# First stage of a split Fourier transform: one product over two batches, or four products in the quarters of PE

## The chip, the cores and the metric

The kernel runs on one core of a Trainium2 chip. The metric is the device time of one execution in microseconds. A core has TensorE (PE, matrix products into PSUM), VectorE (DVE), ScalarE (ACT), GpSimd (POOL) and SyncE (SP), each with an instruction queue of its own, and 16 DMA engines that the queues of SP, POOL and ACT feed. SBUF and PSUM have 128 partitions; PSUM has 8 banks of 512 f32 numbers per partition.

## The reference

```python
X = np.fft.fft(x, axis=1)            # x: (8, 3008, 256) f32
X = np.fft.fft(X, axis=2)
x = X.real.reshape(24064, 256)
h = x @ w_in                         # (256, 2048)
g = h * np.clip(h + 3.0, 0.0, 6.0) / 6.0
out = g @ w_out                      # (2048, 256)
```

## The kernel before

**The transform.** The sequence of 3008 = 47 x 64 is transformed in two stages: 47-point transforms down the columns n1 (first stage, `stage1`), then 64-point ones with the twiddle factors in the table (`stage2`). The transform over the 256 columns is folded into `w_in`. The 8 batches go in 4 pairs. Before the first stage the input is folded by symmetry (`fold`: rows with their partners, columns with theirs), so that 32 of the 64 values of n2 are left. They come in 8 chunks of 4 (`XC`); the last chunk (index 7, the first in the order of pair 0) also holds n2 = 0 and 32 and is computed from two half products.

**First stage.** A chunk's rows lie on 94 partitions (`PR`), the 47 values of n1 of the one batch under those of the other. The table `F` is block-diagonal, 94 x 96: its two 47 x 48 blocks give 24 frequencies with real and imaginary part for each batch (`PZ` = 96). `stage1(pr, c, i)` (lines 199 to 214) is one product of 94 x 96 with 512 columns, two values of n2; it is called for i = 0 and 1. `evict_z` has ScalarE copy each 96 x 512 result from PSUM to `z`, and behind the second one SP stores `z` to DRAM (`zd`, line 243). `turn_column` makes a copy with signs of one column of `z` and stores it to `zq` (257 to 261). For pair 0, `turned_column` computes this column by small products instead. `load_g` reads `zd` and `zq` back, batches on 64 partitions each, for `stage2`.

**Input.** POOL's queue loads a chunk: `load_forward` (line 150) 96 rows in one DMA, and `load_partners` (159) 96 rows of the reversed partners by an indirect DMA. For pair 0 VectorE folds, for the others POOL (lines 170 to 178).

**The start.** Pair 0's 8 chunks are loaded, folded, transformed and stored one after another (lines 685 to 703), each followed by a product with nothing to compute (`keep_awake`, 622). Of `zd` only the first sixth is stored at once (248); the rest waits in `later` and is stored by SP in the first eight steps (853). Then the weights are rebuilt from their stored form by all engines, and folded (593 to 610).

**The steady loop.** 384 steps (4 pairs x 12 chunks of output x 8). Step s issues, in this order on each queue: what `beside` has put at this step; `mlp1` of step s + 2 (line 337: 4 products into the PSUM tiles u and v; VectorE adds and gates at 342 to 358 and 382, ScalarE applies relu at 379); `combine` of step s + 1 (POOL, 396); and `mlp2` of step s (line 422: 7 products by a Strassen-like scheme). `beside(p)` puts the next pair's loads, folds and first-stage products at fixed steps: load at t, the folds at t + 3 and t + 5, the two products at t + 8 and t + 11, with t = 9c for chunk c (t = 8 + 8c beside pair 0). It also puts the second-stage products and `load_g` of this pair.

**Banks.** PSUM is divided by hand: four banks for the accumulators (`ps_a`), three in a ring for u, v and other short tiles (`ps_h`, tag `uv`), and one (`ps_d`, tag `d`) shared by first and second stage. In the start (`starting`) `bank` gives accumulator banks instead. The order of instructions is the program's own (`manual_schedule`); each engine works its queue off in order.

Of the kernel before, what the change touches and what calls it, by code (L numbers as in the profile page):

```python
# [58 lines left out]
def kernel(  # L59
# [17 lines left out]
    PR, PZ = 2 * N1, 4 * NK1  # L77
    XC = 4
# [32 lines left out]
    F = consts.tile([PR + 2, 6 * PZ], F32, name="F")  # L111
    FI = consts.tile([PR + 2, NP * NXC + 1], F32, name="FI")
    IX = consts.tile([PR + 2, NP * NXC], I32, name="IX")
# [19 lines left out]
    def x_tile(pr, c):  # L133
        pool, tag = (spool, "t") if pr.p == 0 and ORDER.index(c) % 3 == 2 else (xpool, "x")
        return pool.tile([PR + 2, XC, D], F32, tag=tag, name="xt")
# [8 lines left out]
    def load_forward(pr, c):  # L144
        xt = x_tile(pr, c)

        nr = PR + 2 if pr.p < NP - 1 else PR
        rows = x_pn[pr.p * PR:pr.p * PR + nr]
        n = XC if c < NXC - 1 else XC - 1
        nc.gpsimd.dma_start(out=xt[0:nr, 0:n, :], in_=rows[:, c * XC + 1:c * XC + 1 + n, :])  # L150
        if n < XC:
            nc.gpsimd.dma_start(out=xt[0:nr, n:XC, :], in_=rows[:, 0:1, :])
        pr.x[c] = xt

    def load_partners(pr, c):
        xr = x_tile(pr, c)
        pr.xr[c] = xr
        i = pr.p * NXC + c
        nc.gpsimd.indirect_dma_start(
            out=xr[:].rearrange("p n d -> p (n d)"), out_offset=None, in_=x_r,  # L160
            in_offset=bass.IndirectOffsetOnAxis(ap=IX[:, i:i + 1], axis=0),
        )

    def fold(pr, c, part, eng):
        xt, xr = pr.x[c][0:PR], pr.xr[c][0:PR]
        n = XC if c < NXC - 1 else XC - 1
        a, r = xt[:, 0:n, :], xr[:, XC - 1:(XC - 1 - n) if n < XC else None:-1, :]
        tt = eng.tensor_tensor
        if part == 0:
            tt(a[:, :, 1:P], a[:, :, 1:P], r[:, :, D - 1:P:-1], op=AL.add)  # L170
            tt(a[:, :, D - 1:P:-1], a[:, :, D - 1:P:-1], r[:, :, 1:P], op=AL.add)
            return
        y = ypool.tile([PR, XC + 1, D], F32, tag="y", name="y")
        pr.y[c] = y
        lo, hi = xt[:, :, 1:P], xt[:, :, D - 1:P:-1]
        tt(y[:, 0:XC, 1:P], lo, hi, op=AL.add)
        tt(y[:, 0:XC, P + 1:D], lo, hi, op=AL.subtract)
        tt(y[:, 0:n, 0:P + 1:P], a[:, :, 0:P + 1:P], r[:, :, 0:P + 1:P], op=AL.add)
        if n < XC:
            h = xr[:, 0, :]  # L180
            tt(y[:, XC, 1:P], h[:, 1:P], h[:, D - 1:P:-1], op=AL.add)
            tt(y[:, XC, P + 1:D], h[:, 1:P], h[:, D - 1:P:-1], op=AL.subtract)
            eng.tensor_copy(y[:, XC, 0:P + 1:P], h[:, 0:P + 1:P])
            eng.tensor_copy(y[:, n, 0:P + 1:P], xt[:, n, 0:P + 1:P])
        del pr.x[c], pr.xr[c]
# [13 lines left out]
    def stage1(pr, c, i):  # L199

        y = pr.y[c]
        pt = turned_column(pr, c, y) if pr.p == 0 and i == 0 else None
        ps = bank([P, 2, D], "ps1")
        if (c, i) == (NXC - 1, XC // 2 - 1):


            nc.tensor.matmul(ps[0:PZ, 0], F[0:PR, 0:PZ], y[:, 2 * i], start=True, stop=False, skip_group_check=True)
            for k, (j, cs) in enumerate([(XC - 1, slice(0, P + 1)), (XC, slice(0, P + 1)),
                                         (XC - 1, slice(P + 1, D)), (XC, slice(P + 1, D))]):
                nc.tensor.matmul(ps[0:PZ, 1, cs], F[0:PR, (k + 1) * PZ:(k + 2) * PZ], y[:, j, cs],  # L210
                                 start=False, stop=(k % 2 == 1), skip_group_check=True)
        else:
            nc.tensor.matmul(ps[0:PZ], F[0:PR, 0:PZ], y[:, 2 * i:2 * i + 2, :], start=True, stop=True)  # L213
        evict_z(pr, c, i, ps, pt)


    def turned_column(pr, c, y):
        n = XC if c < NXC - 1 else XC - 1
        pt = ps_h.tile([P, 2 * TB], F32, tag="uv", name="pt")
        nc.tensor.matmul(pt[0:PZ, 0:n], F[0:PR, 5 * PZ:6 * PZ], y[:, 0:n, P], start=True, stop=True)  # L220
        for k in range(2 if n < XC else 0):
            nc.tensor.matmul(pt[0:PZ, n:XC], F[0:PR, (k + 1) * PZ:(k + 2) * PZ], y[:, n + k, P:P + 1],
                             start=(k == 0), stop=(k == 1))
        return pt

    def evict_z(pr, c, i, ps, pt):
        if i == 0:
            k = ORDER.index(c) if pr.p == 0 else 0

            pool, tag = (zpool, "z") if k < 2 else (cpool, "c") if k < 5 else (qpool, "q") if k < 7 else (apool, "a")  # L230
            pr.z[c] = pool.tile([PZ, XC, DZ[pr.p > 0]], F32, tag=tag, name="z")
            if pr.zd is None:
                pr.zd = dpool.tile([NG, 2, 2 * KK, 2, NS, DZ[pr.p > 0]], F32, tag=f"zd{pr.p > 0}", name="zd")
                pr.zq = dpool.tile([NG, 2, 2 * KK, 2, NS], F32, tag="zq", name="zq") if pr.p > 0 else None
        z = pr.z[c]
        if pt is not None:
            nc.scalar.copy(z[:, :, D], pt[0:PZ, 0:XC])
        nc.scalar.copy(z[:, 2 * i:2 * i + 2, 0:D], ps[0:PZ])
        if i == XC // 2 - 1:
            zd = pr.zd[:].rearrange("g b k c n d -> (g b k c) n d")[:, c * XC:(c + 1) * XC, :]  # L240
            del pr.y[c], pr.z[c]
            if pr.p > 0:
                nc.sync.dma_start(out=zd, in_=z[:])
                turn_column(pr, c, z)
            else:

                n0 = PZ // NG
                nc.sync.dma_start(out=zd[0:n0], in_=z[0:n0])
                later.append((zd[n0:], z[n0:]))
# [4 lines left out]
    def turn_column(pr, c, z):  # L254
        n = XC if c < NXC - 1 else XC - 1
        zc = zpool.tile([PZ, XC], F32, tag="zc", bufs=4, name="zc")
        nc.scalar.activation(zc[:, 0:n], z[:, 0:n, P], AF.Identity, scale=FI[0:PZ, NP * NXC:])
        cs = slice(c * XC, c * XC + n)
        nc.sync.dma_start(out=pr.zq[:, :, :, ::-1, cs].rearrange("g b k c n -> (g b k) c n"), in_=zc[:, 0:n])
        if n < XC:  # L260
            nc.sync.dma_start(out=pr.zq[:, :, :, :, c * XC + n].rearrange("g b k c -> (g b k c)"), in_=z[:, n, P])


    def load_g(pr, gr):
        g = gpool.tile([P, 2 * KK, D + 1], F32, tag="g", name="g")
        gb = [g[b * N2:(b + 1) * N2] for b in range(2)]
        for b in range(2):
            nc.sync.dma_start(out=gb[b][:, :, 0:DZ[pr.p > 0]], in_=pr.zd[gr, b].rearrange("k c n d -> (c n) k d"))
        for b in range(2) if pr.p > 0 else ():
            nc.sync.dma_start(out=gb[b][:, :, D], in_=pr.zq[gr, b].rearrange("k c n -> (c n) k"))  # L270
        pr.g[gr] = g
# [356 lines left out]
    nc.sync.dma_start(out=FI[:], in_=c_stage1[:, 6 * PZ:])  # L628
    nc.sync.dma_start(out=F[:], in_=c_stage1[:, 0:6 * PZ])
# [57 lines left out]
    for k, c in enumerate(ORDER):  # L687
        for part in range(2):
            fold(first, c, part, nc.vector)
        for i in range(XC // 2):  # L690
            stage1(first, c, i)
# [47 lines left out]
    def beside(p):  # L739
        at = {}  # L740

        def put(t, f, *a):
            at.setdefault(t, []).append((f, a))
# [19 lines left out]
        if p + 1 < NP:  # L763
            nx = pairs[p + 1]
            for c in range(NXC):
# [4 lines left out]
                for i in range(XC // 2):  # L770
                    put(t + 8 + 3 * i, stage1, nx, c, i)
# [3 lines left out]
        return at  # L775
# [62 lines left out]
    for s, (p, ck, fc) in enumerate(steps):  # L838
        if ck == 0 and fc == 0:
            at = beside(p)  # L840
        for f, a in at.get(ck * NF + fc, ()):
            f(*a)
        if s < NF:
# [8 lines left out]
            for dst, src in later[2 * s:2 * s + 2]:  # L852
# [10 lines left out]
        else:  # L863
            if s + AHEAD < len(steps):
                mlp1(*chunk(s + AHEAD))
            if s + 1 < len(steps):
# [14 lines left out]
def _tables(B, S, D):  # L881
# [14 lines left out]
    f = np.zeros((2, N1, 6, 2, NK1, 2))  # L896
    for b in range(2):
        for i, (re, im) in enumerate([(co, si), (co, o), (o, co2), (si, o), (o, si2), (-si, co)]):
            f[b, :, i, b, :, 0], f[b, :, i, b, :, 1] = re, im
    f[:, :, 2:5:2] = f[:, ::-1, 2:5:2]  # L900
    f = f.reshape(2, N1, 6, 2, NK1 // 4, 4, 2).swapaxes(3, 4)
# [3 lines left out]
    rows = np.arange(2)[:, None] * N1 + np.arange(N1)[::-1]  # L905
    rows = (rows.reshape(-1, 1) + 2 * N1 * np.arange(B // 2)) * 2 * npc
    rows = rows[:, :, None] + 2 * npc - 1 - np.arange(npc)
    f = np.concatenate([f.reshape(2 * N1, -1), rows.reshape(2 * N1, -1)], axis=1)

    f = np.pad(f, ((0, 2), (0, 0)))  # L910
    f = np.concatenate([f, 1.0 - 2.0 * (np.arange(4 * NK1)[:, None] % 2)], axis=1)
# [47 lines left out]
```

## Time and profile before

| what | value |
|---|---|
| median of 3 runs | 1968.65 us (1968.22 to 1968.8) |
| profiled execution, its time | 1967.16 us |
| its span, first to last instruction | 1965.4 us |
| PE clock granted, mean | 0.999 |
| one step of the loop on PE (599.36 to 604.11) | 4.75 us |
| POOL: one load of x, one indirect load (median) | 0.548, 0.956 us |
| ScalarE: one copy of z | 0.582 us |
| data moved | 93.34 MB, mean 47 GB/s |

The busy time of an engine counts the time in which at least one of its instructions runs. PE's records overlap, since its ends are modelled with the way through the array, so the distance between starts tells what a product costs, and the mean length does not. `x120` for line 213 counts two records for each of 60 products. A group's last part is the idle time of its engine just before it, and what ended most of it. In an order of time, the first number is the start in the span, the second the length, with neighbours of one kind merged.

### The profile page before, as it was taken

The page shows a single profiled execution, that of the slowest core. Times are in us where ns is not written, and L with a number is a line of the kernel's source. Part 1 is how long each engine was busy: PE and PEld are TensorE (multiplying, and loading weights), DVE is VectorE, ACT ScalarE, POOL GpSimd, SP SyncE. Part 2 cuts the span into 40 slices and gives each one's busy share as a digit, 9 for nine tenths or more (in the row PEclk, how much of TensorE's full clock was granted, in tenths as well). Part 3 has the DMA queues.
Part 4 walks back from the last instruction along what each step waited for, and adds up shares of the span by engine and source line. Part 5 has one row for each costly group of instructions (what it writes and reads, how often), then busy time and mean ns, then how long its engine had stood idle before and what let it go on. Part 6 is the DMA issues. An engine that isn't in the chain of part 4 may idle for free.

```text
span 1965.4 us, 27617 instructions
## 1 busy us (share of the span) xinstructions
PE 1942.5 (99%) x9134; PEld 1671.3 (85%) x9134; DVE 1437.9 (73%) x2777; ACT 687.9 (35%) x1167; POOL 1399.7 (71%) x1593
## 2 busy tenths in 40 slices
PE   9999999999999999999999999999999999999997
PEld 4678888888998888888898888888889888888887
DVE  6876776767777777777787776777678777777776
ACT  5633333333333333333333333333333333333322
POOL 4077877876677877787668777778667667666764
PEclk9999999999999999999999999999999999999999
DMA  7521212211112122121211221112110101101000
GB/s 232 172 70 37 66 44 62 52 36 35 35 28 51 43 69 54 36 51 27 49 27 37 55 61 35 52 44 54 35 27 20 28 17 23 29 19 28 19 20 20
DMA packets 144701, 93.34 MB, mean 47 GB/s; under 512 B 116743, under 2 KB 130059, under 8 KB 144558
## 3 DMA queue, kind: packets, MB, share of 16 engines
q1 hardware_dynamic: 134294, 57.89, 12.2%
q0 software_dynamic: 9472, 33.49, 5.9%
q8 instruction: 72, 1.18, 0.3%
q14 instruction: 71, 0.58, 0.1%
q10 hardware_dynamic: 792, 0.20, 0.0%
HBM read 54.22 MB, written 37.32 MB: 47 GB/s over the span
## 4 chain that ended last, share of the span: by engine, by line
PE 93%; DVE 3%; DMA 1%; ACT 1%; issue 1%; SPq 0%; DVEq 0%; POOL 0%; ACTq 0%; POOLq 0%
PE acc L422 55%; PE v L337 16%; PE u L337 16%; PE ps L213 2%; PE ps L286 2%; DMA xt<-in_x_dram,IX 1%; DVE a L382 1%; PE acc L406 1%; DVE s L342 1%; ACT t L379 1%; PE spare L593 0%; DVE o L480 0%; DVE u L363 0%; ACT PM L532 0%; DMA T<-in_c_stage_dram 0%
## 5 line engine op out<-in xcount | busy, mean ns | idle before, releaser
L396 POOL TENSOR_TENSOR c<-a 128x512 f32<-128x512 f32 (+1 forms) x375 | 468.4, 1249 | 399.9 <-PE acc L422 335.4
L422 PE MATMUL acc<-c,G 128*128 128x256 f32 (+1 forms) x3008 | 696.9, 374 | 0.0
L379 ACT ACTIVATE t<-u,half 128x512 f32<-128x512 f32 (+1 forms) x384 | 261.3, 681 | 1099.3 <-DVE u L352 1019.6
L422 PEld LDWEIGHTS acc<-c,G 128*128 128x128 f32 x3008 | 565.4, 190 | 71.1
L342 DVE SCALAR_TENSOR_TENSOR s<-qn,WN,u 128x256 f32<-128x256 f32 (+1 forms) x768 | 330.3, 471 | 353.1 <-PE u L337 352.6
L422 PE MATMUL acc<-a,G 128*128 128x256 f32 (+1 forms) x2256 | 538.8, 374 | 0.0
L422 PEld LDWEIGHTS acc<-a,G 128*128 128x128 f32 x2256 | 423.3, 190 | 55.0
L337 PE MATMUL v<-q,W 127*128 127x256 f32 (+1 forms) x1536 | 389.0, 375 | 2.6 <-DVE a L382 2.6
L337 PE MATMUL u<-q,W 128*128 128x256 f32 (+1 forms) x1536 | 387.9, 375 | 0.0
L382 DVE SCALAR_TENSOR_TENSOR a<-t,u 128x512 f32<-128x512 f32 (+2 forms) x448 | 263.8, 601 | 103.0 <-ACT t L379 98.7
L337 PEld LDWEIGHTS u<-q,W 128*128 128x128 f32 x1536 | 285.8, 190 | 56.1 <-issue 15.8
L337 PEld LDWEIGHTS v<-q,W 127*128 127x128 f32 x1536 | 288.1, 190 | 42.8 <-ACT t L379 2.7
L396 POOL TENSOR_TENSOR c<-a,c 128x256 f32<-128x256 f32 (+1 forms) x375 | 268.8, 717 | 29.4
L396 POOL TENSOR_TENSOR c<-c,a 128x256 f32<-128x256 f32 (+1 forms) x375 | 268.3, 715 | 29.4
L352 DVE TENSOR_TENSOR u<-s,v 128x512 f32<-128x512 f32 x352 | 245.0, 696 | 37.0 <-DVE s L342 0.5
L382 DVE SCALAR_TENSOR_TENSOR a<-t,v 128x512 f32<-128x512 f32 (+1 forms) x480 | 263.7, 566 | 0.5 <-ACT t L379 0.4
L379 ACT ACTIVATE t<-v,half 128x512 f32<-128x512 f32 (+1 forms) x384 | 261.3, 681 | 0.6 <-PE acc L422 0.4
L354 DVE TENSOR_TENSOR v<-v,s 128x512 f32<-128x512 f32 x352 | 244.0, 693 | 0.0
L396 POOL TENSOR_TENSOR r<-w,e 128x256 f32<-128x256 f32 (+1 forms) x92 | 88.8, 986 | 3.6
L430 ACT ACTIVATE e<-acc 128x512 f32<-128x512 f32 (+2 forms) x186 | 84.6, 546 | 3.4 <-PE acc L422 3.3
L480 DVE STREAM_TRANSPOSE o<-r 128x256 f32<-128x256 f32 (+1 forms) x192 | 72.5, 415 | 0.2
L213 PE MATMUL ps<-y,F 94*96 94x512 f32 x120 | 61.3, 601 | 5.2 <-ACT q L289 5.2
(97 smaller groups left out, 794.8 us busy)
## 6 DMA issues: line engine op xcount, KB each, us to landing
out_dram<-o SPq DMA_DIRECT2D x746, 32.0 KB
zd<-z SPq DMA_DIRECT2D x24, 384.0 KB
g<-zd SPq DMA_DIRECT2D x36, 256.0 KB
xt<-in_x_dram POOLq DMA_DIRECT2D x21, 384.0 KB, 4.2
qn<-qd SPq DMA_DIRECT2D x19, 256.0 KB
st<-in_moe_w_in_dram POOLq DMA_DIRECT2D x8, 512.0 KB, 8.0
st<-in_moe_w_out_dram POOLq DMA_DIRECT2D x8, 512.0 KB, 5.6
g<-zd SPq DMA_DIRECT2D x12, 257.0 KB
```

The source lines that it names most:

```text
L213: nc.tensor.matmul(ps[0:PZ], F[0:PR, 0:PZ], y[:, 2 * i:2 * i + 2, :], start=True, stop=True)
L286: nc.tensor.matmul(ps[:, blk, u * P:n].rearrange("p (b k) -> p b k", b=2), g[:, kk, blk * (P + 1):blk * (P + 1) + P], T[:, :, gr, blk, kk, ...
L337: nc.tensor.matmul(ps[:, i, 0:nq], W1[r, blk, f * P:(f + 1) * P], q[r, blk, of:of + nq], start=True, stop=True)
L342: nc.vector.scalar_tensor_tensor(s[:, i, 0:nq], qn[:, of:of + nq], WN[:, f:f + 1], u[:, i, 0:nq], op0=AL.mult, op1=AL.add)
L352: nc.vector.tensor_tensor(u[:], s[:], v[:], op=AL.add)
L354: nc.vector.tensor_tensor(v[:], v[:], s[:], op=AL.subtract)
L379: nc.scalar.activation(t, h, AF.Relu, bias=half[:], scale=scale)
L382: nc.vector.scalar_tensor_tensor(dst, t, 1.0, h, op0=AL.min, op1=AL.mult)
L396: (eng or nc.gpsimd).tensor_tensor(out, in0, in1, op=AL.add)
L422: nc.tensor.matmul(ch.acc[i // 2][:, i % 2, 0:ch.n], G[:, i, fc, :], mv, start=(fc == 0 and i % 2 == 0), stop=(fc == NF - 1), skip_group_c ...
L430: nc.scalar.mul(ch.e[:, k:i + 1, 0:ch.n], ch.acc[i // 2][:, 0:i + 1 - k, 0:ch.n], 1.0 / WS)
L480: nc.vector.transpose(o[:, 0:n // DH, h], ch.r[:, m, h, 0:n].rearrange("p (j i) -> p j i", i=DH))
```

## The change

Each batch of a pair now lies on 64 partitions of its own (rows 0 to 46, and 64 to 110), and the table is the 47 x 48 block alone, once for each batch, padded to 64 columns. The first stage of a chunk is four products, two batches (b, by rows) times two halves of the chunk (h, by columns of the array): each takes 47 partitions and 64 columns, a quarter of PE, with 512 moving columns. Batch b has a PSUM bank of its own, in which half h fills 64 partitions. ScalarE still copies two results for each chunk, now 112 x 512 each, one for each batch. The second bank is a slot of the `uv` ring.

- `stage1` is called once for a chunk, at t + 8, and behind `mlp1` of the step where it was in front (`behind`).
- The forward load is two DMAs, 64 and 48 rows; the indirect load takes 112 rows (96 before). The 17 rows between the batches are loaded and folded but in no product.
- The stores of `z` are two for each chunk, one for each half, with pieces of two n2 (2 KB) in place of four; so are those of `zq` and the deferred ones in `later` (16 of 40 rows for 8 of 80; the same steps).
- `turned_column` is four small products for one. `zd` and `zq` have the batch in another place of their layout.

```diff
-    PR, PZ = 2 * N1, 4 * NK1
+    PB, PZ = P // 2, 2 * NK1
+    PX = PB + N1 + 1
...
+        for b in range(2):
+            i = 2 * pr.p + b
+            nr = N1 + 1 if i < B - 1 else N1
+            if b == 0:
+                nr = PB
+            rows, o = x_pn[i * N1:i * N1 + nr], xt[b * PB:b * PB + nr]
+            nc.gpsimd.dma_start(out=o[:, 0:n, :], in_=rows[:, c * XC + 1:c * XC + 1 + n, :])
...
-    def stage1(pr, c, i):
-        ps = bank([P, 2, D], "ps1")
...
-            nc.tensor.matmul(ps[0:PZ], F[0:PR, 0:PZ], y[:, 2 * i:2 * i + 2, :], start=True, stop=True)
-        evict_z(pr, c, i, ps, pt)
+    def stage1(pr, c):
+        y = pr.y[c]
+        pt = turned_column(pr, c, y) if pr.p == 0 else None
+        ps = [bank([P, 2, D], "ps1"),
+              bank([P, 2, D], "ps1") if starting[0] else ps_h.tile([P, 2, D], F32, tag="uv", name="ps1")]
+        for h in range(2):
+            last = (c, h) == (NXC - 1, 1)
+            for b in range(2):
+                n = 1 if last else 2
+                nc.tensor.matmul(ps[b][h * PB:(h + 1) * PB, 0:n], F[rows(b), 0:PB], y[rows(b), 2 * h:2 * h + n],
+                                 start=True, stop=not last, skip_group_check=last)
+            cosine, sine = slice(0, P + 1), slice(P + 1, D)
+            for k, (j, cs) in enumerate([(XC - 1, cosine), (XC, cosine), (XC - 1, sine), (XC, sine)] if last else ()):
+                for b in range(2):
+                    nc.tensor.matmul(ps[b][h * PB:(h + 1) * PB, 1, cs], table(k + 1, b), y[rows(b), j, cs],
+                                     start=False, stop=(k % 2 == 1), skip_group_check=True)
+        evict_z(pr, c, ps, pt)
+
+    def rows(b):
+        return slice(b * PB, b * PB + N1)
...
+        for b in range(2):
+            if pt is not None:
+                nc.scalar.copy(z[:, b, :, D], pt[b][0:PB + PZ, 0:2])
+            nc.scalar.copy(z[:, b, :, 0:D], ps[b][0:PB + PZ])
+        n0 = PZ // NG if pr.p == 0 else PZ
+        for h in range(2):
+            cs = slice(c * XC + 2 * h, c * XC + 2 * h + 2)
+            zd = pr.zd[:].rearrange("b g k c n d -> (g k c) b n d")[:, :, cs, :]
+            nc.sync.dma_start(out=zd[0:n0], in_=z[h * PB:h * PB + n0])
+            if n0 < PZ:
+                later.append((zd[n0:], z[h * PB + n0:h * PB + PZ]))
...
-                for i in range(XC // 2):
-                    put(t + 8 + 3 * i, stage1, nx, c, i)
+                put(t + 8, stage1, nx, c, at=behind)
...
-            for dst, src in later[2 * s:2 * s + 2]:
+            for dst, src in later[4 * s:4 * s + 4]:
...
             if s + AHEAD < len(steps):
                 mlp1(*chunk(s + AHEAD))
+            for f, a in behind.get(ck * NF + fc, ()):
+                f(*a)
             if s + 1 < len(steps):
                 combine(*chunk(s + 1))
```

More of the change, by code (lines that the diff above doesn't have):

```diff
@@ L109 @@
     ctx.enter_context(tc.manual_schedule())
-    F = consts.tile([PR + 2, 6 * PZ], F32, name="F")
-    FI = consts.tile([PR + 2, NP * NXC + 1], F32, name="FI")
-    IX = consts.tile([PR + 2, NP * NXC], I32, name="IX")
+    F = consts.tile([P, 6 * PB], F32, name="F")
+    FI = consts.tile([P, NP * NXC + 1], F32, name="FI")
+    IX = consts.tile([P, NP * NXC], I32, name="IX")
     T = consts.tile([P, 2, NG, 2, 2 * KK, N2], F32, name="T")
@@ L134, in x_tile @@
         pool, tag = (spool, "t") if pr.p == 0 and ORDER.index(c) % 3 == 2 else (xpool, "x")
-        return pool.tile([PR + 2, XC, D], F32, tag=tag, name="xt")
+        return pool.tile([PX, XC, D], F32, tag=tag, name="xt")
     def load_x(pr, c):
@@ L145, in load_forward @@
         xt = x_tile(pr, c)
-        nr = PR + 2 if pr.p < NP - 1 else PR
-        rows = x_pn[pr.p * PR:pr.p * PR + nr]
         n = XC if c < NXC - 1 else XC - 1
-        nc.gpsimd.dma_start(out=xt[0:nr, 0:n, :], in_=rows[:, c * XC + 1:c * XC + 1 + n, :])
-        if n < XC:
-            nc.gpsimd.dma_start(out=xt[0:nr, n:XC, :], in_=rows[:, 0:1, :])
+        for b in range(2):
[5 more added lines that the diff above has]
+            nc.gpsimd.dma_start(out=o[:, 0:n, :], in_=rows[:, c * XC + 1:c * XC + 1 + n, :])
+            if n < XC:
+                nc.gpsimd.dma_start(out=o[:, n:XC, :], in_=rows[:, 0:1, :])
         pr.x[c] = xt
@@ L160, in load_partners @@
             out=xr[:].rearrange("p n d -> p (n d)"), out_offset=None, in_=x_r,
-            in_offset=bass.IndirectOffsetOnAxis(ap=IX[:, i:i + 1], axis=0),
+            in_offset=bass.IndirectOffsetOnAxis(ap=IX[0:PX, i:i + 1], axis=0),
         )
     def fold(pr, c, part, eng):
-        xt, xr = pr.x[c][0:PR], pr.xr[c][0:PR]
+        xt, xr = pr.x[c][0:PX - 1], pr.xr[c][0:PX - 1]
         n = XC if c < NXC - 1 else XC - 1
@@ L172, in fold @@
             return
-        y = ypool.tile([PR, XC + 1, D], F32, tag="y", name="y")
+        y = ypool.tile([PX - 1, XC + 1, D], F32, tag="y", name="y")
         pr.y[c] = y
@@ L197, in bank @@
         return ps_d.tile(shape, F32, tag="d", name=name)
-    def stage1(pr, c, i):
+    def stage1(pr, c):
         y = pr.y[c]
-        pt = turned_column(pr, c, y) if pr.p == 0 and i == 0 else None
-        ps = bank([P, 2, D], "ps1")
[L204 to L213, printed above, removed]
-        evict_z(pr, c, i, ps, pt)
@@ L217, in turned_column @@
-    def turned_column(pr, c, y):
[L218 to L223, printed above, removed]
-        return pt
[L226 to L249, printed above, removed]
@@ L254, in turn_column @@
-    def turn_column(pr, c, z):
[L255 to L261, printed above, removed]
+        pt = turned_column(pr, c, y) if pr.p == 0 else None
@@ new lines, in stage1, with table @@
+        evict_z(pr, c, ps, pt)
+    def rows(b):
+        return slice(b * PB, b * PB + N1)
+    def table(i, b):
+        return F[rows(b), i * PB:(i + 1) * PB]
+    def turned_column(pr, c, y):
+        pt = [ps_h.tile([P, 2 * TB], F32, tag="uv", name="pt") for b in range(2)]
+        for h in range(2):
+            last = (c, h) == (NXC - 1, 1)
+            n = 1 if last else 2
+            for b in range(2):
+                o = pt[b][h * PB:(h + 1) * PB]
+                nc.tensor.matmul(o[:, 0:n], table(5, b), y[rows(b), 2 * h:2 * h + n, P], start=True, stop=True)
+                for k in range(2 if last else 0):
+                    nc.tensor.matmul(o[:, 1:2], table(k + 1, b), y[rows(b), XC - 1 + k, P:P + 1],
+                                     start=(k == 0), stop=(k == 1))
+        return pt
@@ new lines, in evict_z @@
+    def evict_z(pr, c, ps, pt):
+        k = ORDER.index(c) if pr.p == 0 else 0
+        pool, tag = (zpool, "z") if k < 2 else (cpool, "c") if k < 5 else (qpool, "q") if k < 7 else (apool, "a")
+        dz = DZ[pr.p > 0]
+        z = pool.tile([PB + PZ, 2, 2, dz], F32, tag=tag, name="z")
+        if pr.zd is None:
+            pr.zd = dpool.tile([2, NG, 2 * KK, 2, NS, dz], F32, tag=f"zd{pr.p > 0}", name="zd")
+            pr.zq = dpool.tile([NG, 2 * KK, 2, NS, 2], F32, tag="zq", name="zq") if pr.p > 0 else None
+        for b in range(2):
+            if pt is not None:
+                nc.scalar.copy(z[:, b, :, D], pt[b][0:PB + PZ, 0:2])
+            nc.scalar.copy(z[:, b, :, 0:D], ps[b][0:PB + PZ])
+        n0 = PZ // NG if pr.p == 0 else PZ
+        for h in range(2):
+            cs = slice(c * XC + 2 * h, c * XC + 2 * h + 2)
[3 more added lines that the diff above has]
+                later.append((zd[n0:], z[h * PB + n0:h * PB + PZ]))
+        del pr.y[c]
+        if pr.p > 0:
+            turn_column(pr, c, z)
@@ new lines, in turn_column @@
+    def turn_column(pr, c, z):
+        zc = zpool.tile([PB + PZ, 2, 2], F32, tag="zc", bufs=4, name="zc")
+        nc.scalar.activation(zc[:].rearrange("p n b -> p b n"), z[:, :, :, P], AF.Identity,
+                             scale=FI[0:PB + PZ, NP * NXC:])
+        for h in range(2):
+            n = 1 if (c, h) == (NXC - 1, 1) else 2
+            cs = slice(c * XC + 2 * h, c * XC + 2 * h + n)
+            nc.sync.dma_start(out=pr.zq[:, :, ::-1, cs].rearrange("g k c n b -> (g k) c (n b)"),
+                              in_=zc[h * PB:h * PB + PZ, 0:n].rearrange("p n b -> p (n b)"))
+            if n < 2:
+                nc.sync.dma_start(out=pr.zq[:, :, :, NS - 1].rearrange("g k c b -> (g k c) b"),
+                                  in_=z[h * PB:h * PB + PZ, :, 1, P])
@@ L267, in load_g @@
         for b in range(2):
-            nc.sync.dma_start(out=gb[b][:, :, 0:DZ[pr.p > 0]], in_=pr.zd[gr, b].rearrange("k c n d -> (c n) k d"))
+            nc.sync.dma_start(out=gb[b][:, :, 0:DZ[pr.p > 0]], in_=pr.zd[b, gr].rearrange("k c n d -> (c n) k d"))
         for b in range(2) if pr.p > 0 else ():
-            nc.sync.dma_start(out=gb[b][:, :, D], in_=pr.zq[gr, b].rearrange("k c n -> (c n) k"))
+            nc.sync.dma_start(out=gb[b][:, :, D], in_=pr.zq[gr, :, :, :, b].rearrange("k c n -> (c n) k"))
         pr.g[gr] = g
@@ L627 @@
     keep_awake(9)
-    nc.sync.dma_start(out=FI[:], in_=c_stage1[:, 6 * PZ:])
-    nc.sync.dma_start(out=F[:], in_=c_stage1[:, 0:6 * PZ])
+    nc.sync.dma_start(out=FI[:], in_=c_stage1[:, 6 * PB:])
+    nc.sync.dma_start(out=F[:], in_=c_stage1[:, 0:6 * PB])
     bias = wpool.tile([P, 2], F32, tag="bias", name="bias")
@@ L689 @@
             fold(first, c, part, nc.vector)
-        for i in range(XC // 2):
-            stage1(first, c, i)
+        stage1(first, c)
         keep_awake(1)
@@ L739, in beside, with put @@
     def beside(p):
-        at = {}
-        def put(t, f, *a):
+        ahead, behind = {}, {}
+        def put(t, f, *a, at=ahead):
             at.setdefault(t, []).append((f, a))
@@ L769, in beside @@
                 put(t + 5, fold, nx, c, 1, nc.gpsimd)
-                for i in range(XC // 2):
-                    put(t + 8 + 3 * i, stage1, nx, c, i)
+                put(t + 8, stage1, nx, c, at=behind)
             put(NST * (NG - 1) - 2, load_g, nx, 0)
@@ L774, in beside @@
             s2(NST * (NG - 1), nx, 0)
-        return at
+        return ahead, behind
     def close_w():
@@ L839 @@
         if ck == 0 and fc == 0:
-            at = beside(p)
-        for f, a in at.get(ck * NF + fc, ()):
+            ahead, behind = beside(p)
+        for f, a in ahead.get(ck * NF + fc, ()):
             f(*a)
@@ L895, in _tables @@
     o = np.zeros_like(co)
-    f = np.zeros((2, N1, 6, 2, NK1, 2))
-    for b in range(2):
[L898 to L901, printed above, removed]
-    npc = N2 // 8
[L905 to L911, printed above, removed]
+    f = np.zeros((N1, 6, 2, NK1))
+    for i, (re, im) in enumerate([(co, si), (co, o), (o, co2), (si, o), (o, si2), (-si, co)]):
+        f[:, i, 0], f[:, i, 1] = re, im
+    f[:, 2:5:2] = f[::-1, 2:5:2]
+    f = f.swapaxes(2, 3).reshape(N1, 6, -1)
+    npc = N2 // 8
+    t = np.zeros((2, 64, 6 * 64 + B // 2 * npc + 1))
+    t[:, :, -1] = 1.0 - 2.0 * (np.arange(64) % 2)
+    for b in range(2):
+        t[b, :N1, :6 * 64] = np.pad(f, ((0, 0), (0, 0), (0, 64 - f.shape[2]))).reshape(N1, -1)
+        row = ((2 * np.arange(B // 2) + b) * N1 + np.arange(N1)[::-1, None]) * 2 * npc
+        t[b, :N1, 6 * 64:-1] = (row[:, :, None] + 2 * npc - 1 - np.arange(npc)).reshape(N1, -1)
+    f = t.reshape(128, -1)
     k = k1[:, None] + N1 * np.arange(N2)
```

## The prediction

> **What bounds the kernel now.** I read the page's busy times and its chain first, then the groups, then the order of time on PE round one first-stage product, then the start.
>
> ```profile
> PE 1942.5 (99%) x9134; PEld 1671.3 (85%) x9134; DVE 1437.9 (73%) x2777; ACT 687.9 (35%) x1167; POOL 1399.7 (71%) x1593
> ...
> PE 93%; DVE 3%; DMA 1%; ACT 1%; issue 1%; SPq 0%; DVEq 0%; POOL 0%; ACTq 0%; POOLq 0%
> ...
> L213 PE MATMUL ps<-y,F 94*96 94x512 f32 x120 | 61.3, 601 | 5.2 <-ACT q L289 5.2
> ```
>
> PE is busy 99% of the span and 93% of the chain: behind the start, a microsecond of PE time is a microsecond of the kernel. The first stage (L213) is 61.3 us of PE in 120 records, and PE idles 5.2 us before it, for ScalarE to empty the one bank of the `d` pool that the second stage (L289) has filled.
>
> PE in order of time, in the second pair, and beside it the weight loads:
>
> ```profile
> 607.78 1.24 PE L422 MATMUL acc<-c,G 128*128 128x256 f32 x5
> 608.87 1.02 PE L213 MATMUL ps<-y,F 94*96 94x512 f32 x2
> 609.73 1.03 PE L337 MATMUL u<-q,W 128*128 128x256 f32 x4
> ```
> ```profile
> 608.65 0.38 PEld L213 LDWEIGHTS ps<-y,F 94*96 94x96 f32 x2
> 609.30 0.19 PEld L337 LDWEIGHTS u<-q,W 128*128 128x128 f32 x1 [0.27 <-issue]
> ```
>
> The first number is the start. One product of the program is two records, each with a weight load of its own (x2): PE works an f32 product off in two passes. From 608.87 to 609.73 the two passes take 0.86 us, so one pass over 512 columns holds PE for 0.43 us, though its record lasts 0.592 us: the last 0.16 us is the way through the array, under the next pass. A weight load lies under the pass before it (609.30, as the second pass begins).
>
> The start is another regime. Its chain, in order of time, and the busy times of its first 36 us:
>
> ```profile
> 3.00 4.99 DMA xt<-in_x_dram,IX
> ...
> 12.12 5.21 DMA xt<-in_x_dram,IX
> ...
> 21.29 6.46 DMA xt<-in_x_dram,IX
> ...
> 30.74 0.30 PE pt L220 x2
> 31.05 1.79 PE ps L213 x4
> 32.84 0.86 PE awake L622 x2
> 33.70 0.14 PE pt L220 x2
> 33.84 1.81 PE ps L213 x4
> ```
> ```profile
> 0.00:36.00 36.00, 33.52 (x94) 15.12 (x95) 25.76 (x57) 17.57 (x28) 16.00 (x25) 1.00 0.92 264
> ```
>
> The DMA share is 0.92 here (second number from the end): transfers of x, VectorE's folds and PE take turns as the bound. PE works a chunk off every 2.75 us (15.97 to 18.72, and so on), with no idle time from 15.97 to 29.7.
>
> **The change, part by part.** The numbers are against the profiled execution, 1967.16 us (span 1965.4); the median of the three runs, 1968.65, is 1.49 above it, and I add that at the end.
>
> *The products.* Pairs 1 to 3 make 24 chunks beside the saturated PE; pair 0's eight lie in the start. A chunk is now two products, four passes, 4 x 0.43 = 1.72 us. The last chunk of a pair has 0.86 for the first product and (L207 and L210, 13.80 to 15.11 in the start) 1.31 for the rest, 2.17. Together 21 x 1.72 + 3 x 2.17 = 42.6 us. Afterwards a chunk is four products on 64 rows and 64 columns, eight passes of the same 512 columns: twice the passes, so the gain hangs on how many run at once. No operation of this trace uses a part of the array. If the four quarters run side by side, each needs its own two passes, 0.86 us, in the last chunk 1.3: 21 x 0.86 + 3 x 1.3 = 22.0, **-20.6 us**. If nothing overlaps, 21 x 3.44 + 3 x 4.3 = 85.1, +42.5.
>
> Here two statements of the Trainium skill pull apart, both on the page "TensorE: Matmul & The Clock Gate", Part 3. Its section on measured speedup gives products in different tiles a span of one product plus about 4 ns for each further tile: my -20.6. Its section on the mechanism says that matmuls start and end strictly in program order. By the trace a product is two passes through the same quarter, and the change issues the four products one after another; if a waiting second pass holds up all behind it, only the second pass of one product overlaps the first of the next, and eight passes take five: 21 x 5 x 0.43 + 3 x 2.3 = 52.0, +9.4 us, a loss. I take the first: an order of starts need not mean that a pass for a free quarter waits until a busy one is free, and the page's sixteen-tile figure (10.6 times) comes from the packing itself. No row decides it, so the second is my main rival.
>
> *Entering and leaving quarters.* "TensorEngine Tiling (Array Packing)", Key Properties, says that changing the tiling mode drains PE. The nearest row is the 0.16 us of tail on a record. One tail in and one out: 24 x 0.32 = **+7.7 us**. From below 0, if none shows; from above twice that, 15.4, if each switch also uncovers a weight load (0.163 to 0.19 us).
>
> *The waits for the bank.* The products go from in front of the next hidden product (mlp1) to behind it, once per chunk where they were in two places, and the second batch takes a slot of the three-slot `uv` ring. Where a second stage falls in the same step, mlp1's 1.73 us now lie between the two, over the 0.59 us copy. So the 5.2 us go: **-5.2**, bound 0. The new wait is for the `uv` slot, last read by the gate of the previous step's v: at 604.28 in the step that began at 599.36, while the quarter products behind the next mlp1 would start at 605.84. Margin 1.5 us: 0. Queued behind a wait there would be mlp2 (14 passes). On ScalarE the two copies stay two (0.58 us each), behind the step's relus; the extra ring slot comes round in time, since gate ends are 4.3 and 4.9 us after the start of u and their slots are wanted 5.6 and 6.5 us after it. What gets late next is nothing that I can name.
>
> *POOL and SP beside the loop.* Each chunk issues one more load of x, 0.548 us on POOL (L150): 24 x 0.55 = 13 us, under the 335.4 us in which POOL's combine waits for PE:
>
> ```profile
> POOL c L396 <- PE acc L422: 335.4, 191, 4.1
> ```
>
> Folds keep their columns and take 111 rows for 94. SP issues two more small stores a chunk (0.4 us each); SP mostly waits for results to store. Both 0; without the cover, at most 13 and 24 x 2 x 0.4 = 19 us.
>
> *The start.* Both transfers of x grow from 96 rows to 112, a sixth. On the chain they take 4.99 + 5.21 + 6.46 = 16.7 us: +2.8. The extra POOL issue puts each partner load 0.55 us later, three times on the chain, half hidden by full engines: +0.8. The last chunk's end on PE comes 0.5 earlier. The deferred stores (L853, median 0.585 us on SP) double; four more stand before the next table load: 2.3 us, half of it counted, +1.2. Sum **+4.3**, bounds 0 and +7.
>
> Total: -20.6 + 7.7 - 5.2 + 4.3 = -13.8. 1967.16 - 13.8 = 1953.4, and with 1.49: **1955 us**. With the bounds: -25.8 (1943) to +1.8 (1970).
>
> **The rivals.** *Program order holds passes up* (ends slower; place: PE in each of the 24 chunks). +9.4 + 7.7 - 5.2. In the start PE becomes the bound: 0.4 for the small products, 2.15, 0.32 and 0.86 (awake) are 3.73 us a chunk for 2.75; eight from 12.4 end at 42.2 for 35.5: +6.7, and +1.2 of SP. Sum +19.8: **1988**. It decides for slower once a chunk takes over about 1.9 us with the switches. For it: the two records per product, and the page's rule. Against: the same page's packed spans.
>
> *Half the overlap*: the two row halves run together, the two column halves in turn. Four passes as now: 0 + 7.7 - 5.2 + 4.8 = +7.3, **1976**. For it: both column halves read the same rows of y.
>
> *It doesn't do what it says*: the quarters run one after another. +42.5 + 7.7 - 5.2, and the start at 5.0 us a chunk, +16.9 + 1.2: +63, **2032**. The trace has no quarter, so can't exclude it; little speaks for it.
>
> **How the numbers follow.** Four quarters at once 0.77, half the overlap 0.08, program order 0.12, no overlap 0.03. Faster means below 1964.7, slower above 1972.6 (0.2%, about what a measurement of this kernel can tell from no change). Of the first, 0.74 is faster and 0.03 within; of half the overlap 0.03 is within and 0.05 slower; the others are slower. So 0.74, 0.06, 0.20. The likeliest case alone spans 1943 to 1970; with half the overlap the range is 1943 to 1980, about 0.8.
>
> **What would show it.** On PE in order of time, from the start of the first quarter record of a chunk to the next whole-array record: about 1.2 us if right, 2.15 or more by program order, near 2 by half the overlap, over 3.4 without overlap. A gap before the first quarter record and one behind the last are the switches: 0.16 us each. The row of waits for L289 before the first stage should be gone, with none for the `uv` ring in its place. In the start, the last copy to z (35.67 now) should come about 3 us later. Wrong most of all if a quarter record starts only when the product before it is over.

## The result, and the profile after

| | before | after |
|---|---|---|
| median (runs) | 1968.43 us (4) | 1956.66 us (4; 1954.48 to 1957.24) |
| profiled execution | 1967.16 us | 1956.28 us |
| its span | 1965.4 us | 1954.5 us |

The ratio of the times is 0.9938, 95% interval 0.9921 to 0.9955: faster by 12 us, forecast 14.

The page of the changed kernel: busy times, and the chain's shares by engine and by line.

```profile
PE 1931.4 (99%) x9346; PEld 1656.6 (85%) x9346; DVE 1438.3 (74%) x2777; ACT 681.8 (35%) x1175; POOL 1420.4 (73%) x1629
...
PE 93%; DVE 3%; ACT 1%; DMA 1%; issue 1%; POOL 0%; DVEq 0%; SPq 0%; ACTq 0%
PE acc L448 56%; PE v L363 16%; PE u L363 16%; PE ps L312 2%; PE ps L217 1%; DMA xt<-in_x_dram,IX 1%; DVE a L408 1%; PE acc L432 1%; DVE s L368 1%; ACT t L405 1%; ACT PM L558 0%; PE spare L619 0%; DVE o L506 0%; DVE u L389 0%; ACT ex L573 0%
```

The shape is the same; the first stage (now L217) has gone from 2% of the chain to 1%. PE in order of time round one chunk of the second pair, and its weight loads:

```profile
595.17 1.03 PE L363 MATMUL v<-q,W 127*128 127x256 f32 x4
596.13 1.09 PE L217 MATMUL ps<-y,F 47*64 47x512 f32 x8
597.14 1.56 PE L448 MATMUL acc<-a,G 128*128 128x256 f32 x6
598.54 1.67 PE L448 MATMUL acc<-c,G 128*128 128x256 f32 x7
```
```profile
594.95 0.84 PEld L363 LDWEIGHTS v<-q,W 127*128 127x128 f32 x4
596.12 0.21 PEld L217 LDWEIGHTS ps<-y,F 47*64 47x64 f32 x8 [0.33 <-issue]
597.14 1.16 PEld L448 LDWEIGHTS acc<-a,G 128*128 128x128 f32 x6 [0.81 <-issue]
```

Eight passes of 512 columns lie within 1.09 us, and their eight weight loads within 0.21 us: all four quarters start at once. In a window that opens at 596.9, when the first passes are over, only the second four are left, and they start at 596.61:

```profile
596.61 0.61 PE L217 MATMUL ps<-y,F 47*64 47x512 f32 x4
```

So each quarter is held by its first pass for about as long as a pass holds the whole array (0.43 us in the kernel before), and then takes its second. From the first v record to the first combined product (`acc<-c`) is 598.54 - 595.17 = 3.37 us. The same stretch without a chunk is 608.05 - 605.89 = 2.16 us:

```profile
605.89 1.03 PE L363 MATMUL v<-q,W 127*128 127x256 f32 x4
606.75 1.46 PE L448 MATMUL acc<-a,G 128*128 128x256 f32 x6
608.05 1.89 PE L448 MATMUL acc<-c,G 128*128 128x256 f32 x8
```

A chunk costs 1.21 us of PE for 1.72: 0.86 of streaming and 0.35 of switching. The switches can be seen. Without a chunk, v holds PE for 0.86 us (605.89 to 606.75), so here it should be through at about 596.03 (an estimate from that distance); the quarters start at 596.13. The next whole-array product comes at 597.14, 1.01 us after them for 0.86 of streaming, and its weight load starts only together with it; PEld had nothing to do for 0.81 us before. The six passes behind take 1.40 us for 1.30. That is 0.10, 0.15 and 0.10 us.

What PE waits for behind the start, from 130 us on, in the kernel before and in the changed one:

```profile
PE ps L213 <- ACT q L289: 5.2, 8, 0.7
PE v L337 <- DVE a L382: 1.0, 5, 0.2
```
```profile
PE v L363 <- DVE a L408: 0.8, 4, 0.2
```

The row of the bank is gone, and the `uv` ring has given none in its place.

The row of before understates what its waits cost, mainly since it counts idle time only from the modelled end of the record ahead. The distances between starts tell it. This is one of the eight places in the kernel before:

```profile
170.53 1.05 PE L286 MATMUL ps<-T,g 128*128 128x128 f32 x8
172.25 1.10 PE L213 MATMUL ps<-y,F 94*96 94x512 f32 x2 [0.68 <-ACT q L289]
173.19 1.03 PE L337 MATMUL u<-q,W 128*128 128x256 f32 x4
```

Where u follows at once, the eight passes of the second stage hold PE for 0.89 us (35 of 37 times behind 117 us), and a first-stage product holds it for 0.86. Here both take 173.19 - 170.53 = 2.66 us, 0.91 more. Six of the eight places are like this one; in the two like that at 1386.53 it is 0.76. Together that is 7.0 us, for the row's 5.2.

The start got worse. Its chain in the changed kernel, and 22 us of it in both kernels (first before, then after; the last two numbers are the DMA share and GB/s, the one ahead of them PE's granted clock):

```profile
6.25 5.89 DMA xt<-in_x_dram,IX
...
16.62 6.50 DMA xt<-in_x_dram,IX
...
27.58 9.14 DMA xt<-in_x_dram,IX
```
```profile
12.00:34.00 22.00, 21.13 (x73) 9.89 (x72) 18.55 (x37) 9.43 (x22) 10.06 (x13) 1.00 0.96 277
```
```profile
12.00:34.00 22.00, 17.80 (x125) 5.87 (x122) 13.28 (x25) 7.78 (x24) 13.59 (x19) 0.83 1.05 247
```

The DMA engines are full in both, but move 247 GB/s for 277. The three transfers on the chain take 21.5 us for 16.7, and PE, now with idle time between the chunks, is granted 0.83 of its clock.

One cut shows the balance. The last time that PE waits for long (1.5 us, for DVE) before the loop runs free is in front of the same v product in both kernels:

```profile
117.25 1.13 PE L337 MATMUL v<-q,W 127*128 127x256 f32 x4 [1.54 <-DVE a L382]
125.54 1.13 PE L363 MATMUL v<-q,W 127*128 127x256 f32 x4 [1.53 <-DVE a L408]
```

The start lost 125.54 - 117.25 = 8.3 us. From there to the end of the span it is 1965.4 - 117.25 = 1848.15 us before and 1954.5 - 125.54 = 1828.96 after, a gain of 19.2: together -10.9, as the profiled executions differ.

### The profile page after: what moved, and what is told of

It is laid out like the page before. It is cut to its first block, busy times and chain, and to the rows that moved or that the text cites. A ratio compares the mean times of both kernels' runs of the same rounds, so it can differ in the third digit from the quotient of the medians.

```text
span 1954.5 us, 28154 instructions
## 1 busy us (share of the span) xinstructions
PE 1931.4 (99%) x9346; PEld 1656.6 (85%) x9346; DVE 1438.3 (74%) x2777; ACT 681.8 (35%) x1175; POOL 1420.4 (73%) x1629
## 4 chain that ended last, share of the span: by engine, by line
PE 93%; DVE 3%; ACT 1%; DMA 1%; issue 1%; POOL 0%; DVEq 0%; SPq 0%; ACTq 0%
PE acc L448 56%; PE v L363 16%; PE u L363 16%; PE ps L312 2%; PE ps L217 1%; DMA xt<-in_x_dram,IX 1%; DVE a L408 1%; PE acc L432 1%; DVE s L368 1%; ACT t L405 1%; ACT PM L558 0%; PE spare L619 0%; DVE o L506 0%; DVE u L389 0%; ACT ex L573 0%
## 5 line engine op out<-in xcount | busy, mean ns | idle before, releaser
L422 POOL TENSOR_TENSOR w<-w,e 128x512 f32<-128x512 f32 (+1 forms) x46 | 57.5, 1250 | 3.6
```

The costliest lines, as they stand in the source:

```text
L422: (eng or nc.gpsimd).tensor_tensor(out, in0, in1, op=AL.add)
```

## The experiments

Times are compared with the kernel before on the same chip. The start spreads by a microsecond or two from one execution to the next, at times by more: the eighth fold starts at 37.8 in the profile of the changed kernel and at 40.1 in that of `ahead`, whose start is the same, and the kernel before ran in 1966.38 to 1972.26 us on one chip. So differences of one microsecond need more than the medians. The part behind the v product above hardly spreads: in every run whose loop is that of the changed kernel it is within 0.4 us of 1829.

**Do the quarters run side by side, and what if their passes stand in a bad order?** `twice_turn` issues the four full products of a chunk, and then all four again; `twice_row` issues each of them twice in a row.

```diff
+        for h in range(2) if pr.p > 0 and c < NXC - 1 else ():
+            for b in range(2):
+                nc.tensor.matmul(ps[b][h * PB:(h + 1) * PB], F[rows(b), 0:PB], y[rows(b), 2 * h:2 * h + 2],
+                                 start=True, stop=True)
```
```diff
-                nc.tensor.matmul(ps[b][h * PB:(h + 1) * PB, 0:n], F[rows(b), 0:PB], y[rows(b), 2 * h:2 * h + n],
...
+                for twice in range(2 if pr.p > 0 and c < NXC - 1 else 1):
+                    nc.tensor.matmul(ps[b][h * PB:(h + 1) * PB, 0:n], F[rows(b), 0:PB], y[rows(b), 2 * h:2 * h + n],
...
```

The first cut is the edit of `twice_turn`, the second that of `twice_row`.

> The changed kernel with the four full products of a chunk issued twice, all four and then all four again (21 chunks beside the saturated PE; the result is the same). Theory (four quarters side by side): one more round of 0.86 us each, +18.1 us. By program order with passes held up: +1.7 us or more for each, over +36. No overlap: +72.

> The changed kernel with each of the four full products issued twice in a row, so that four passes for one quarter stand one behind the other in the queue. If PE keeps work waiting for a busy quarter while it starts work for free ones: +18.1 us like twice_turn. If passes start in program order and a waiting pass holds up all behind it, at most the last pass of one quarter overlaps the first of the next: 13 passes of 0.43 us for 16, 5.6 us a chunk against 1.2 now, +90 us. In between: the depth of the queue that PE looks through.

1974.09 us (1.0029, interval 1.0018 to 1.0040) and 1974.50 us (1.0030, 1.0019 to 1.0041): 17.4 and 17.8 above the changed kernel's 1956.66, by the profiled spans 18.3 and 18.6. One chunk in `twice_turn` and in `twice_row`:

```profile
602.42 1.09 PE L215 MATMUL ps<-y,F 47*64 47x512 f32 x8
603.33 1.04 PE L221 MATMUL ps<-y,F 47*64 47x512 f32 x8
604.30 1.56 PE L452 MATMUL acc<-a,G 128*128 128x256 f32 x6
```
```profile
602.42 1.97 PE L218 MATMUL ps<-y,F 47*64 47x512 f32 x16
604.32 1.56 PE L449 MATMUL acc<-a,G 128*128 128x256 f32 x6
```

Sixteen passes take 1.88 us in the one order and 1.90 in the other, where starts in program order would take 5.6 in the second. A round without a switch costs 0.87 us (the same stretch from v is 4.24 us for 3.37), the two passes of one quarter. In `twice_row` a window from 602.4 to 602.8 holds four passes:

```profile
602.42 0.68 PE L218 MATMUL ps<-y,F 47*64 47x512 f32 x4
```

All four start in the first 0.04 us, before any quarter is free again, so each is the first pass of another quarter, and that of the last quarter has gone ahead of nine passes that wait for the other three. So four quarters run at once, and a pass that waits for its busy quarter does not hold up those behind it. This falsifies the main rival, and with it half the overlap (near 2 us a chunk) and none (over 3.4).

**What was the move behind the hidden product worth?**

```diff
-                put(t + 8, stage1, nx, c, at=behind)
+                put(t + 8, stage1, nx, c)
```

> The changed kernel with the quarter products in front of the next hidden product again (the step and everything else as in the change). Theory (the move behind it removed the wait for the bank that the second stage has filled, 5.2 us in the kernel before): the wait comes back at those chunks whose step also has a second stage, two in each of pairs 1 and 2, each 0.7 us or more, and at the uv ring where the slot is not yet free; time 1 to 6 us above the changed kernel. Rival (the move is worth nothing, the single call per chunk removed the waits): within 1 us.

1959.25 us (0.9953, interval 0.9939 to 0.9966), 2.6 above the changed kernel. The intervals overlap; the profile decides. From the v product of the cut (127.47 here) to the end of the span (1959.1) it is 1831.6 us for 1828.96: the loop is 2.7 us longer. The waits behind 130 us:

```profile
PE ps L217 <- ACT q L315: 2.5, 4, 0.7
```

Four waits came back of the eight. So the move behind the hidden product is worth 2.7 of the 7.0 us. The rest must have gone with the second place of the products in the loop (the call at t + 11); no run put that back alone.

**Where did the start lose 8.3 us?** First the padding: 17 or 18 partitions of an indirect load all read row 0.

```diff
+        t[b, N1:, 6 * 64:-1] = t[b, :64 - N1, 6 * 64:-1]
```

> The changed kernel, but the 17 padding partitions of each batch get distinct rows of x in the indirect load, instead of all reading row 0 (17 or 18 reads of the same 4 KB in each load). The numbers loaded there are in no product. Theory A (the start lost 8.3 us since 18 reads of one row hold the indirect load up): the indirect loads get shorter, the eighth fold ends 2 to 5 us earlier than 40.5, time 2 to 5 us below the changed kernel's 1956.66, about 1953. Theory B (the loss is the sixth more bytes and the extra issues alone): no change, within 1 us.

1956.14 us (0.9937, interval 0.9923 to 0.9950): theory A fell. Its start is no shorter (the eighth fold starts at 39.1). Next PE's clock:

```diff
-        keep_awake(1)
+        keep_awake(3)
```

> The changed kernel with three empty products behind each chunk of the start instead of one, so that PE has no long idle time there. Theory C (PE's idle time of up to 2.9 us between the chunks of the start takes its clock down, 0.55 to 0.82 in the profile, and slows the last chunks and the weight work behind them by 1.2 us): granted clock 1.0 in the start, last fold to first weight product 8.5 us in place of 9.8, time 1 us lower, 1955.5. Rival: the lower clock costs nothing, as transfers bound the start; then the extra empty products only delay the last chunk, by 1 to 2 us.

1955.26 us (0.9934, 0.9921 to 0.9948), which the time alone can't tell from the changed kernel. The profiles can. From the start of the eighth fold to the second group of the weight products (`wps`) it is 30.64 to 41.93 before (11.3 us), 37.77 to 50.23 after (12.5) and 37.99 to 49.17 here (11.2). Twelve microseconds of the start, after and in `awake3`:

```profile
36.00:48.00 12.00, 10.99 (x43) 3.56 (x44) 5.94 (x13) 6.00 (x14) 0.00 (x0) 0.55 0.61 204
```
```profile
36.00:48.00 12.00, 11.12 (x55) 4.29 (x55) 7.10 (x15) 7.13 (x16) 0.00 (x0) 1.00 0.71 226
```

The clock is back from 0.55 to 1.00, and with it 1.2 us. The other profiles with the changed kernel's start (`spread_pad`, `ahead`, `twice_turn`, `twice_row`) have a clock of 0.52 to 0.61 in this stretch and 12.0 to 12.5 us. The clock is not all that moves this distance: the profile of `b112_hot` below has 12.9 us at 0.92.

Then the rows, put into the kernel before: pair 0 loads 112 rows, its products stay.

```diff
-        nr = PR + 2 if pr.p < NP - 1 else PR
+        nr = 112 if pr.p == 0 else PR + 2 if pr.p < NP - 1 else PR
...
+        m = 112 if pr.p == 0 else PR + 2
...
-            in_offset=bass.IndirectOffsetOnAxis(ap=IX[:, i:i + 1], axis=0),
+            in_offset=bass.IndirectOffsetOnAxis(ap=IX[0:m, i:i + 1], axis=0),
```

> The kernel before, with one part of the change alone: pair 0 loads 112 rows in the forward and in the indirect load (96 before), the padding of the indirect load all from row 0; folds and products stay on 94 rows. Theory A or B (rows cost): the start gets longer by 3 to 6 us, time 1971.5 to 1974.5. If instead the second forward load's issue or the lower clock makes the loss of the start, below 1 us: 1969.

> As b112_hot, with the padding of the indirect load spread over distinct rows. Theory A (one row read 18 times): 2 to 5 us less than b112_hot. Theory B (bytes): the same as b112_hot within 1 us, 2.8 to 3.7 us above the kernel before, by 2.1 MB... of which one sixth is 1.05 MB at the 287 GB/s of the start.

1970.94 us (1.0016, interval 1.0010 to 1.0023) and 1970.12 us (1.0012, 1.0006 to 1.0019): 3.5 and 2.6 us above the 1967.48 of the kernel before there. The bytes cost what was expected of them, and the padding's rows again make no difference beyond the intervals. Some four microseconds of the 8.3 were still open. The last part is the cut of the forward load, added to `b112_spread`:

```diff
-        nc.gpsimd.dma_start(out=xt[0:nr, 0:n, :], in_=rows[:, c * XC + 1:c * XC + 1 + n, :])
+        for r in ((slice(0, 64), slice(64, 112)) if pr.p == 0 else (slice(0, nr),)):
+            nc.gpsimd.dma_start(out=xt[r, 0:n, :], in_=rows[r, c * XC + 1:c * XC + 1 + n, :])
```

> As b112_spread, with pair 0's forward load cut into two DMAs of 64 and 48 rows, as in the change (the same bytes; products and folds of the kernel before). Theory D (the rest of the start's loss beyond the rows comes with the cut of the forward load: its second issue on POOL, 0.55 us a chunk, and the transfers' rate, 240 GB/s in the first 45 us for 253 with one load): 3 to 5 us above b112_spread's 1970.1, about 1974, and the eighth fold's start near 37. Rival E (the cut is free, the rest comes from PE's lower clock and from the smaller stores of z): 1970, as b112_spread.

1974.60 us (1.0034, interval 1.0022 to 1.0046), 7.0 above the kernel before there (1967.62): some 4 us more for the same bytes in two DMAs (the interval of `b112_spread` lies below this one). The same 22 us in `b112_spread` and in `b112_split`:

```profile
12.00:34.00 22.00, 18.73 (x60) 8.08 (x60) 16.50 (x31) 8.27 (x20) 10.33 (x14) 1.00 1.03 282
```
```profile
12.00:34.00 22.00, 17.23 (x56) 7.47 (x57) 14.13 (x27) 7.32 (x17) 13.76 (x19) 0.99 1.04 251
```

The engines are full in both, and the rate falls from 282 to 251 GB/s, near the changed kernel's 247. It is so in every profile of this case: in this stretch the four kernels with one forward load move 277 to 282 GB/s, with 96 rows as with 112, and the seven with the cut load 237 to 251. Why two DMAs of 64 and 48 rows move less than one of 112 at the same share, these runs don't show.

By the v product of the cut in the profiles, the rows cost 2.8 us (117.25 to 120.07 in `b112_spread`) and the cut 3.7 (to 123.76 in `b112_split`); with 1.2 for the clock that is 7.7 of the 8.3. The rest is within the spread. The smaller stores of `z` and the small products of the start were not put back alone.

**The loop of the changed kernel with the start of the kernel before.** Pair 0 keeps its 94 x 96 products, single loads and stores; pairs 1 to 3 have the quarters.

```diff
-        stage1(first, c)
+        for i in range(XC // 2):
+            stage1_0(first, c, i)
...
+        if pr.p == 0:
+            rows = x_pn[0:PR0 + 2]
+            nc.gpsimd.dma_start(out=xt[0:PR0 + 2, 0:n, :], in_=rows[:, c * XC + 1:c * XC + 1 + n, :])
...
+            put(6, load_f)
```

> The changed kernel for pairs 1 to 3, and the kernel before for pair 0: its loads of 96 rows, 94 x 96 products, stores and deferred stores; the second table is loaded in step 6. Theory (the gain is all in the 24 chunks beside the saturated PE, the loss all in the start): the start of before and the loop of after, 19.2 us below the kernel before, 1949. Rival (the start's loss comes back later, as work that the longer start hid): 1953 or more.

1948.36 us (0.9902, interval 0.9887 to 0.9918), 19.3 below the kernel before: the forecast to a microsecond, and faster than both. With the start of before, the loop keeps its whole gain of 19 us, so the longer start had hidden no work that comes back later.

## Why the prediction was right

The mechanism, the place and the sign held, and the sizes of the loop to 2 us a term; the start was mis-sized.

- *The products*: forecast 42.6 to 22.0 us and 7.7 us of switches, -12.9. Measured 21 chunks at 1.21 and 3 last ones at 1.67 (by the same distance from v), 30.4: -12.2. The switch is 0.35 us a chunk for my 0.32, but in other parts than mine: I had two tails of 0.16, and the rows have 0.10 in front, 0.15 beyond the streaming before the next array product, with its weight load uncovered, and 0.10 in the passes behind. That the sum came so close is in part luck. "TensorEngine Tiling (Array Packing)" of the Trainium skill, Key Properties, says that a change of mode drains PE; the 0.10 and 0.15 us agree with it, but with modelled ends the rows can't show whether PE was empty.
- *The choice between the two rules* of "TensorE: Matmul & The Clock Gate" of the Trainium skill, Part 3: the packed span is right here (four products in 1.01 us, where one holds PE for 0.86), and my reading of program order as a hold-up is not. `twice_row` shows it, with 1.90 us for 5.6; the profile of before could not. The 0.12 for that rival and 0.77 for the packing were a judgement, not a result.
- *The waits*: forecast -5.2, the row's idle time; the row is gone. By the distances between starts in the kernel before, six waits held PE for 0.91 us and two for 0.76: -7.0. With the products this is -19.2, the whole gain of the loop. So the products gained 0.7 us less than forecast, and the waits 1.8 more.
- *The start*: forecast +4.3, measured +8.3, just outside my bound of 7. The term that failed is the transfers: "a sixth" of 16.7 us, +2.8, took the rate as given. The transfers on the chain took 4.8 us more, since the cut load also lowered the rate; I had the cut as 0.8 us of issue on POOL, and it cost about 4. The rows alone were sized right: 2.6 to 3.5 us. I also had no term for PE's clock, which fell once PE had idle time in the start: +1.2. And I had +1.2 for the deferred stores, which cost nothing: the delay is 8.3 us at 50.23 (41.93 before) and still 8.3 at 125.54.
- *POOL and SP beside the loop* at 0: held, since PE waits 0.8 us in all behind 130 us.

The errors of the start (4 us too little cost) and of the loop (1 us too little gain) partly cancel; that much of the closeness of the total is luck.

## What to carry to other kernels

Four products of at most 64 rows and 64 columns, one for each quarter of PE, stream in the time of one: here 0.86 us, half of the 1.72 that the two larger products took in their place. One entry into the quarters and the return together cost 0.35 us here, so put such products in one place and keep whole-array work out from between. A layout that suits PE may be paid for elsewhere: padding rows and cutting loads cost nothing that shows where PE was the bound, and 7 us where the transfers were. Read what a wait costs from the distances between starts: the row of idle time gave 5.2 us for 7.0. Cost a change separately in each regime of the kernel, and change the layout only where it pays: the hybrid keeps the 19 us and loses none of them.

## What the runs showed of the hardware that was not expected

- The two passes of an f32 product in one quarter don't hold up passes for other quarters: sixteen passes in either order take 1.88 and 1.90 us, with four in a row for one quarter in the second.
- The same bytes in two DMAs of 64 and 48 rows moved at 251 GB/s, in one of 112 rows at 282, with the DMA engines full both times. All eleven profiles fall into these two groups (237 to 251, 277 to 282).
- In the changed kernel's start PE sat idle for 1.4, 2.4 and 2.9 us between bursts (ending at 18.87, 31.31 and 36.95), and its granted clock was 0.82, 0.78 and 0.55 in the three stretches of 12 us from 12 us on. With two more empty products a chunk the longest idle time up to 60 us was 0.8 us, and the clock stayed at 1.00. One idle time of 1.5 us, at 117 us in the kernel before, did not lower it. Which length matters, these runs don't show.
